# Gated attention and feed-forward decode: a piece of one wq block moves from the 128-partition stream to eight four-partition DMAs, and the stream's buffers get another start address

## The chip, the cores and the metric

The kernel runs on one core of a Trainium2 chip. A core has the engines PE (TensorE, matmul), DVE (VectorE), ACT (ScalarE), POOL (GpSimd) and SP (SyncE), and 16 DMA engines that bring data from device memory (HBM) to the core's memory (SBUF, 128 partitions). The metric is the time of one execution in device microseconds (us). The time before is 812.78 us, the median of 3 runs (812.65 to 812.88).

## The reference, cut to what matters

One token `x` of 1024 numbers goes through two branches, and a sigmoid gate mixes them. All numbers are float32.

```python
q = x @ wq                      # 1024 -> 32 heads of 128
scores = q @ k.T * 128 ** -0.5  # 4 kv heads, 65536 cached keys each; 8 query heads share a kv head
o = softmax(scores) @ v
a = o @ wo                      # 4096 -> 1024
y = (silu(x @ w_gate) * (x @ w_up)) @ w_down      # 1024 -> 3584 -> 1024
b = x + y * sigmoid(x @ w_r)
out = g * a + (1 - g) * b       # g = sigmoid(sum(x * gate_w))
```

Every weight and every cached key and value is used once, for one token: some 346 MB are read and 4 KB are written.

## The kernel before, in words

All large inputs are laid out on the host as one stream, in the order in which they are used: for each of the four kv heads g its part of wq (`q`), its keys, its values and its part of wo, then w_gate, w_up and w_down. In each of the 128 partitions the stream has `TOTAL` = 675,840 floats. It is cut into 48 loads: a first one of `FIRST` = 2048 columns, a tensor of its own (`flow0`), and 47 of `LOAD` = 14,336 columns (57,344 bytes in each partition, 7,340,032 bytes in all) from `flow`.

`at(part, first, n)` (L88) gives the SBUF columns that hold a stretch of the stream. When the load that holds it hasn't been asked for, it takes the next of the three buffers of the pool `stream` (L71) and issues the load on SP (L95 for the first, L99 for the others). A load into a buffer waits until PE has read all of the buffer's former content, so up to three loads are on the way or in use. SP issues nothing else but the store of the result (L293). The last two loads are cut into two and six pieces (`ENDS`, L51), so that PE can begin on the first columns.

A DMA of a load writes all 128 partitions. Between HBM and SBUF a partition's columns of one DMA are contiguous on both sides.

The work on a load is matmuls with the streamed data as the moving operand, 32 output rows at a time in four row groups j:

- `queries(g)` (L150): 8 blocks k of wq, 4 matmuls of 256 columns each (L154), with the columns of `xp` as weights. The result goes through `q_sb` (L159) and two small matmuls with `sel4` (L162) into `qp` (L164).
- `score_chunk` (L169): 16 matmuls of 512 columns for a chunk of 8192 keys (L173), ACT's copy (L178), DVE's maximum (L179). `neg_max` (L182) makes the softmax's offset from the 8 chunks, with a matmul of its own (L189).
- `value_chunk` (L197): ACT's exponential (L198), DVE's transpose (L200), 16 matmuls (L203). `project` (L208) scales and multiplies by wo (L226).
- `up_proj` (L242) for w_gate and w_up (L249), then w_down (L280, and L287 for the last block in two pieces), the last vector operation (L292) and the store.

The tile framework orders the instructions of each engine and sets the waits. The pool `const` holds the small tiles that live for the whole kernel; the three buffers of `stream` come behind it in each partition, so the size of `const` sets where they begin. The sizes in `const` are those of the tiles in the listing, each rounded up to 32 bytes: `xk` (L79) has 3 x 8 floats, 96 bytes. POOL does nothing but make `ident` (L106), from which DVE makes `sel`, `sel8`, `sel4` (L111 to L117). ACT issues the two small loads of `xk` and `x_row`; the latter writes four partitions, 0, 32, 64 and 96 (L84).

Of the kernel before, what the change touches and what calls it, by code (L numbers as in the profile page):

```python
# [1 line left out]

# [6 lines left out]
F32 = mybir.dt.float32  # L9
# [4 lines left out]
P = 128  # L14
D = 1024
G = 4
# [6 lines left out]
NM = CH // 512  # L23
NB = CH // P
KB = D // P
NQ = D // 4
FB = F // P
FQ = FB // 4
# [3 lines left out]
LOAD = 14336  # L32
PARTS = [("q", 0, KB * D)]
for _g in range(G):
    PARTS += [("k", _g, NCH * CH), ("v", _g, NCH * CH), ("o", _g, HG * D)]
    if _g < G - 1:
        PARTS.append(("q", _g + 1, KB * D))
PARTS += [("gate", 0, KB * F), ("up", 0, KB * F), ("down", 0, FB * D)]
BEGIN = {}
TOTAL = 0  # L40
# [1 line left out]
    BEGIN[_n, _g] = TOTAL  # L42
    TOTAL += _l

FIRST = TOTAL % LOAD
NLOAD = TOTAL // LOAD + 1
assert FIRST and (BEGIN["gate", 0] - FIRST) % LOAD == 0

PIECES = [(0, 192), (192, NQ)]

ENDS = {NLOAD - 2: [8 * D, LOAD], NLOAD - 1: [6 * D, 10 * D, 12 * D, 13 * D, 13 * D + 768, LOAD]}  # L51


@with_exitstack
def gated_mix_kernel(ctx: ExitStack, tc: tile.TileContext, x, vecs, flow0, flow, out):

# [10 lines left out]
    nc = tc.nc  # L69
    const = ctx.enter_context(tc.tile_pool(name="const", bufs=1))  # L70
# [5 lines left out]
    ps_1 = ctx.enter_context(tc.tile_pool(name="ps_1", bufs=1, space=bass.MemoryType.PSUM))  # L76


    xk = const.tile([P, 3, KB], F32, name="xk")  # L79
    nc.scalar.dma_start(xk, vecs)  # L80
    x_row = const.tile([P, NQ], F32, name="x_row")
    nc.vector.memset(x_row, 0.0)

    nc.scalar.dma_start(x_row.rearrange("(j r) n -> j r n", r=32)[:, 0, :], x.rearrange("(j n) -> j n", j=4))  # L84

    loads = []

    def at(part, first, n):  # L88

        i, a = divmod(BEGIN[part] + first - FIRST, LOAD)  # L90
        i, a = (i + 1, a) if i >= 0 else (0, BEGIN[part] + first)
        while len(loads) <= i:
            t = stream.tile([P, LOAD], F32, name="st", tag="st")
            if not loads:
                nc.sync.dma_start(t[:, :FIRST], flow0)  # L95
            else:
                ends = ENDS.get(len(loads), [LOAD])
                for c0, c1 in zip([0] + ends, ends):
                    nc.sync.dma_start(t[:, c0:c1], flow[len(loads) - 1, :, c0:c1])  # L99
            loads.append(t)  # L100
        return loads[i][:, a : a + n]

    at(("q", 0), 0, 1)

    ident = const.tile([P, P], F32, name="ident")
# [13 lines left out]

    xp = const.tile([P, KB, 32], F32, name="xp")  # L120
    nc.vector.memset(xp, 0.0)
    nc.vector.tensor_copy(xp[:, :, 0], xk[:, 0, :])

    qp = const.tile([P, 2, 4, 32], F32, name="qp")
    nc.vector.memset(qp, 0.0)
# [5 lines left out]

    dots = const.tile([P, 2, KB], F32, name="dots")
    for i in range(2):
# [3 lines left out]
    ps = ps_1.tile([P, P], F32, name="ps_m", tag="m")  # L137
# [5 lines left out]
    gate = sig[:, 0:1]  # L143
# [3 lines left out]
    nc.vector.tensor_mul(rest[:, 1:2], rest[:, 0:1], sig[:, 1:2])  # L147
    att = ps_1.tile([P, NQ], F32, name="att", tag="att")

    def queries(g):  # L150
        ps = ps_s.tile([P, 512], F32, name="ps_q", tag="s")
        for k in range(KB):
            for j in range(4):
                nc.tensor.matmul(  # L154
                    ps[32 * j : 32 * j + 32, :NQ], xp[:, k, :], at(("q", g), k * D + j * NQ, NQ),
                    start=(k == 0), stop=(k == KB - 1),
                )
        q_sb = work.tile([P, NQ], F32, name="q_sb")
        nc.vector.tensor_copy(q_sb, ps[:, :NQ])  # L159
        pt = ps_1.tile([P, P], F32, name="ps_m", tag="m")  # L160
        for e in range(2):
            nc.tensor.matmul(pt[:, 4 * e : 4 * e + 4], q_sb[:, e * DH : (e + 1) * DH], sel4, start=True, stop=True)  # L162
        for s in range(4):
            nc.vector.tensor_copy(  # L164
                qp[:, g % 2, s, 8 * s : 8 * s + 8].rearrange("p (j e) -> p e j", e=2),
                pt[:, :HG].rearrange("p (e j) -> p e j", e=2),
            )

    def score_chunk(g, c, mx):  # L169
        ps = ps_s.tile([P, 512], F32, name="ps_s", tag="s")  # L170
        for s in range(4):
            for j in range(4):
                nc.tensor.matmul(  # L173
                    ps[32 * j : 32 * j + 32, :], qp[:, g % 2, s, :], at(("k", g), c * CH + (4 * s + j) * 512, 512),
                    start=(s == 0), stop=(s == 3),
                )
        t = scores.tile([P, 512], F32, name="s", tag="s")
        nc.scalar.activation(t, ps, AF.Copy)  # L178
        nc.vector.tensor_reduce(mx[:, c : c + 1], t, AX.X, ALU.max)  # L179
        return t  # L180
# [50 lines left out]
    for g in range(G):  # L231
        queries(g)
        mx = work.tile([P, NCH], F32, name="mx")
        s_t = [score_chunk(g, c, mx) for c in range(NCH)]
        nb = neg_max(mx)
        sums = work.tile([P, NCH], F32, name="sums")
        acc = ps_o.tile([P, 512], F32, name="acc", tag="o")
        for c in range(NCH):
            value_chunk(g, c, s_t[c], nb, sums, acc)
        project(g, acc, sums)  # L240
# [37 lines left out]
    for b in range(FB - 1):  # L278
        for j in range(4):
            nc.tensor.matmul(  # L280
                y[32 * j : 32 * j + 32, :], hp[:, b, :], at(("down", 0), b * D + j * NQ, NQ),
                start=(b == 0), stop=False,
            )
    for c0, c1 in PIECES:
        n = c1 - c0
        for j in range(4):
            nc.tensor.matmul(  # L287
                y[32 * j : 32 * j + 32, c0:c1], hp[:, FB - 1, :], at(("down", 0), (FB - 1) * D + 4 * c0 + j * n, n),
                start=False, stop=(c1 == NQ),
# [39 lines left out]
```

## Time and profile before

| | |
|---|---|
| median of 3 runs | 812.78 us (812.65 to 812.88) |
| the profiled execution, its own time | 812.77 us |
| its span, first to last instruction | 811.0 us |
| instructions | 6755 |
| PE busy | 420.3 us (52%) |
| DVE busy | 64.3 us (8%) |
| ACT busy | 45.6 us (6%) |
| read from HBM | 346.05 MB |

The profile is a page on one execution, and views of its trace. The span leaves out 1.8 us of the execution's time at its ends. "DMA" with digits is the busy share of the 16 DMA engines in 40 slices, in tenths. A DMA queue is named by a number: q1 is SP's, q10 is ACT's, and two queues of kind "instruction" bring the engines' own instructions. The "chain that ended last" goes back from the last instruction, at each step to what released it. A table of windows gives, for each stretch of the span, the busy time of each engine, then the clock granted to PE, the mean busy share of the 16 DMA engines and the rate in GB/s.

### The profile page before, as it was taken

To read this page: it belongs to the slowest core of one execution; us is meant where nothing else is said; L and a number is where in the kernel's file an instruction comes from. 1 tells how busy PE (TensorE), PEld (TensorE's weight loads), DVE (VectorE), ACT (ScalarE), POOL (GpSimd) and SP (SyncE) were. 2 spreads that over 40 slices of the span, in tenths; PEclk is the share of its full clock that TensorE was granted. 3 is DMA by queue.
4 is the path that set the end of the run, shared out by engine and by line. 5 is a ranking of instruction groups with operands and counts; after the bars stand their busy time and mean duration, and the time that the engine had idled before them with its cause. 6 is when DMAs were issued, how large, how long until landed. Compare 5 with 4: busy or idle time off the path is not lost.

```text
span 811.0 us, 6755 instructions
## 1 busy us (share of the span) xinstructions
PE 420.3 (52%) x3142; PEld 127.3 (16%) x3142; DVE 64.3 (8%) x149; ACT 45.6 (6%) x101; POOL 0.7 (0%) x6
## 2 busy tenths in 40 slices
PE   1455454555445564345544545555555544575485
PEld 0111110113101011012110111121111111121132
DVE  2000110000000120000010101000000200000000
ACT  0000020000000020000000300000000200000000
POOL 0000000000000000000000000000000000000000
PEclk9967767678866686666776677767667766677677
DMA  9999999999999999999999999999999999999996
GB/s 415 405 453 419 438 434 424 448 410 448 428 430 439 425 442 422 436 436 422 441 431 436 428 430 436 425 438 442 424 434 428 430 436 427 445 422 436 426 423 276
DMA packets 7963, 346.47 MB, mean 427 GB/s; under 512 B 1016, under 2 KB 1152, under 8 KB 1408
## 3 DMA queue, kind: packets, MB, share of 16 engines
q1 hardware_dynamic: 7784, 346.04, 99.0%
q8 instruction: 24, 0.39, 0.2%
q10 hardware_dynamic: 152, 0.02, 0.0%
q14 instruction: 3, 0.02, 0.0%
HBM read 346.05 MB, written 0.00 MB: 427 GB/s over the span
## 4 chain that ended last, share of the span: by engine, by line
DMA 81%; PE 17%; DVE 1%; issue 0%; SPq 0%; ACT 0%; ACTq 0%
DMA st<-in_flow 81%; PE ps_s L173 7%; PE acc L203 6%; PE ps_f L249 1%; PE ps_q L154 1%; PE att L226 1%; PE ps_m L218 0%; SPq L99 0%; PE ps_m L162 0%; DVE o_sb L214 0%; DVE q_sb L159 0%; ACT s L198 0%; PE ps_m L189 0%; DVE pt L200 0%; DVE mx L179 0%
## 5 line engine op out<-in xcount | busy, mean ns | idle before, releaser
L173 PE MATMUL ps_s<-st,qp 128*32 128x512 f32 x1024 | 154.0, 765 | 150.4 <-DMA st<-in_flow 149.4
L203 PE MATMUL acc<-st,pt 128*32 128x512 f32 x1024 | 155.2, 768 | 140.6 <-DMA st<-in_flow 133.3
L173 PEld LDWEIGHTS ps_s<-st,qp 128*32 128x32 f32 x1024 | 38.2, 136 | 262.1 <-issue 149.1
L203 PEld LDWEIGHTS acc<-st,pt 128*32 128x32 f32 x1024 | 37.3, 136 | 250.7 <-issue 135.4
L178 ACT ACTIVATE s<-ps_s 128x512 f32<-128x512 f32 x32 | 19.1, 597 | 576.7 <-PE ps_s L173 576.7
L249 PE MATMUL ps_f<-st,xp 128*32 128x448 f32 x256 | 34.9, 715 | 26.0 <-DMA st<-in_flow 26.0
L179 DVE TENSOR_REDUCE mx<-s 128x1 f32<-128x512 f32 x32 | 22.0, 686 | 286.4 <-ACT s L178 286.4
L200 DVE STREAM_TRANSPOSE pt<-s 128x512 f32<-128x512 f32 x32 | 22.8, 712 | 191.9 <-PE acc L203 188.2
L154 PE MATMUL ps_q<-st,xp 128*32 128x256 f32 x256 | 23.3, 514 | 18.8 <-DMA st<-in_flow 18.8
L226 PE MATMUL att<-st,op 128*32 128x256 f32 x256 | 20.8, 487 | 13.7 <-DMA st<-in_flow 12.1
L198 ACT ACTIVATE s<-s,nb 128x512 f32<-128x512 f32 x32 | 22.6, 708 | 11.0 <-DVE nb L194 11.0
L280 PE MATMUL y<-st,hp 128*32 128x256 f32 x216 | 16.5, 472 | 5.4 <-DMA st<-in_flow 5.2
L249 PEld LDWEIGHTS ps_f<-st,xp 128*32 128x32 f32 x256 | 9.8, 140 | 50.2 <-issue 27.6
L154 PEld LDWEIGHTS ps_q<-st,xp 128*32 128x32 f32 x256 | 10.0, 144 | 30.7 <-DMA st<-in_flow 20.2
L226 PEld LDWEIGHTS att<-st,op 128*32 128x32 f32 x256 | 9.7, 139 | 23.3 <-DMA st<-in_flow 13.1
L280 PEld LDWEIGHTS y<-st,hp 128*32 128x32 f32 x216 | 7.9, 133 | 13.7 <-DMA st<-in_flow 7.2
L254 ACT ACTIVATE row<-ps_f 128x896 f32<-128x896 f32 x2 | 1.8, 917 | 142.1 <-PE ps_f L249 142.1
L214 DVE COPY o_sb<-acc 128x512 f32<-128x512 f32 x4 | 2.8, 692 | 78.5 <-PE acc L203 78.5
L216 PE MATMUL ps_m<-sel,lb 128*128 128x8 f32 x8 | 1.9, 304 | 10.8 <-DVE lb L212 10.6
L159 DVE COPY q_sb<-ps_q 128x256 f32<-128x256 f32 x4 | 1.7, 425 | 63.6 <-PE ps_q L154 63.6
L189 PE MATMUL ps_m<-md,ones 128*128 128x128 f32 x8 | 2.5, 406 | 8.0 <-DVE md L187 8.0
L218 PE MATMUL ps_m<-sel,o_sb 128*128 128x8 f32 x32 | 5.0, 285 | 2.5 <-DVE o_sb L214 2.5
(55 smaller groups left out, 46.1 us busy)
## 6 DMA issues: line engine op xcount, KB each, us to landing
st<-in_flow SPq DMA_DIRECT2D x45, 7168.0 KB, 42.2
st<-in_flow SPq DMA_DIRECT2D x2, 3072.0 KB, 41.7
st<-in_flow SPq DMA_DIRECT2D x1, 4096.0 KB
st<-in_flow SPq DMA_DIRECT2D x2, 1024.0 KB, 21.9
st<-in_flow SPq DMA_DIRECT2D x1, 2048.0 KB, 36.9
st<-in_flow SPq DMA_DIRECT2D x1, 512.0 KB, 39.7
st<-in_flow SPq DMA_DIRECT2D x1, 384.0 KB, 40.3
st<-in_flow SPq DMA_DIRECT2D x1, 128.0 KB, 34.3
```

The lines of the kernel that those rows point to most:

```text
L154: nc.tensor.matmul(ps[32 * j : 32 * j + 32, :NQ], xp[:, k, :], at(("q", g), k * D + j * NQ, NQ), start=(k == 0), stop=(k == KB - 1),)
L173: nc.tensor.matmul(ps[32 * j : 32 * j + 32, :], qp[:, g % 2, s, :], at(("k", g), c * CH + (4 * s + j) * 512, 512), start=(s == 0), stop=(s ...
L178: nc.scalar.activation(t, ps, AF.Copy)
L179: nc.vector.tensor_reduce(mx[:, c : c + 1], t, AX.X, ALU.max)
L198: nc.scalar.activation(t, t, AF.Exp, bias=nb, scale=SCALE, accum_out=sums[:, c : c + 1])
L200: nc.vector.transpose(pt, t)
L203: nc.tensor.matmul(acc[32 * j : 32 * j + 32, :], pt[:, 32 * m : 32 * m + 32], at(("v", g), c * CH + m * 512, 512), start=(c == 0 and m < 4 ...
L214: nc.vector.tensor_copy(o_sb, acc.rearrange("p (s d) -> p s d", s=4))
L218: nc.tensor.matmul(ps[:, HG : 2 * HG], o_sb[:, s, :], sel[:, HG * s : HG * s + HG], start=(s == 0), stop=(s == 3))
L226: nc.tensor.matmul(att[32 * j : 32 * j + 32, :], op[:, h, :], at(("o", g), h * D + j * NQ, NQ), start=(g == 0 and h == 0), stop=(g == G - ...
L249: nc.tensor.matmul(ps[32 * j : 32 * j + 32, e, :n], xp[:, k, :], at((part, 0), k * F + (2 * j + e) * n, n), start=(k == 0), stop=(k == KB ...
L280: nc.tensor.matmul(y[32 * j : 32 * j + 32, :], hp[:, b, :], at(("down", 0), b * D + j * NQ, NQ), start=(b == 0), stop=False,)
```

## The change: a piece of wq on its own DMAs, and the loads that follow from it

- Of the last kv head's `q`, the first 768 columns of the last block (k = 7) leave the stream: 768 floats in each of 128 partitions, 393,216 bytes. The stream's `TOTAL` is 675,072 then.
- They are folded on the host into the tensor `quarters`, with 4 x 768 floats for each of 32 rows: row p of wq's 128 stands in row 32 * q + r, slot h, with p = 32 h + 16 q + r. In SBUF it is the tile `quart`, 48 partitions of 12,288 bytes, of which rows 0 to 15 and 32 to 47 hold data. POOL sets it to zero first.
- Eight DMAs bring it, each four partitions, four apart (r, r + 4, r + 8, r + 12, and the same 32 further on), 49,152 bytes. SP issues one behind every third load: behind loads 3, 6 and so on up to 24.
- `queries(3)` has 12 matmuls on `quart` in 4 slots, with `xh` as weights, in place of 3 on the stream: 41 matmuls for 32.
- The loads are cut anew (`CUTS`): 2048 columns, then 14,336 each, and 13,568 in the one load that holds the last head's `q`, so that from w_gate on the cuts are where they were. There is one tensor `flow` for all loads, the first included, whose rows are now 57,344 bytes apart.
- `xk` has a fourth vector (128 bytes), and `quart` and `xh` (512 bytes) come to `const`: together 12,832 bytes. The buffers of `stream` begin 12,832 bytes further on, at multiples of 256 bytes.

```diff
+NH = 4
+NC = 768
-        PARTS.append(("q", _g + 1, KB * D))
+        PARTS.append(("q", _g + 1, KB * D - (NC if _g == G - 2 else 0)))
...
-FIRST = TOTAL % LOAD
-NLOAD = TOTAL // LOAD + 1
+CUTS = [0]
+while CUTS[-1] < BEGIN["q", G - 1]:
+    CUTS.append(CUTS[-1] + LOAD if len(CUTS) > 1 else 2 * D)
+CUTS.pop()
+CUTS.append(BEGIN["gate", 0] - (BEGIN["gate", 0] - CUTS[-1]) // LOAD * LOAD)
+while CUTS[-1] < TOTAL:
+    CUTS.append(CUTS[-1] + LOAD)
+NLOAD = len(CUTS) - 1
...
-    xk = const.tile([P, 3, KB], F32, name="xk")
+    xk = const.tile([P, 4, KB], F32, name="xk")
...
+    quart = const.tile([48, NH, NC], F32, name="quart")
+    nc.gpsimd.memset(quart, 0.0)
+    fours = [slice(32 * q + r, 32 * q + r + 13, 4) for q in range(2) for r in range(4)]
...
             t = stream.tile([P, LOAD], F32, name="st", tag="st")
-            if not loads:
-                nc.sync.dma_start(t[:, :FIRST], flow0)
-            else:
-                ends = ENDS.get(len(loads), [LOAD])
-                for c0, c1 in zip([0] + ends, ends):
-                    nc.sync.dma_start(t[:, c0:c1], flow[len(loads) - 1, :, c0:c1])
+            ends = ENDS.get(len(loads), [CUTS[len(loads) + 1] - CUTS[len(loads)]])
+            for c0, c1 in zip([0] + ends, ends):
+                nc.sync.dma_start(t[:, c0:c1], flow[len(loads), :, c0:c1])
             loads.append(t)
+            if len(loads) % 3 == 0 and fours:
+                rows = fours.pop(0)
+                nc.sync.dma_start(quart[rows], quarters[rows])
...
+    xh = const.tile([48, NH, 32], F32, name="xh")
+    nc.vector.memset(xh, 0.0)
+    nc.vector.tensor_copy(xh[:, :, 0], xk[:48, 3, :NH])
...
+        mms = []
+        if g == G - 1:
+            mms = [(j, xh[:, i, :], quart[:, i, j * NQ : (j + 1) * NQ]) for i in range(NH) for j in range(NC // NQ)]
         for k in range(KB):
-            for j in range(4):
-                nc.tensor.matmul(
-                    ps[32 * j : 32 * j + 32, :NQ], xp[:, k, :], at(("q", g), k * D + j * NQ, NQ),
-                    start=(k == 0), stop=(k == KB - 1),
-                )
+            held = NC if g == G - 1 and k == KB - 1 else 0
+            mms += [(j, xp[:, k, :], at(("q", g), k * D + j * NQ - held, NQ)) for j in range(held // NQ, 4)]
```

In the order of PE's instructions, ten of the twelve new matmuls stand behind the last scores of head 2, ahead of that head's `neg_max` matmul (L189 before), and two behind it.

More of the change, by code (lines that the diff above doesn't have):

```diff
@@ L1 @@
+from bisect import bisect
 from contextlib import ExitStack
@@ L43 @@
     TOTAL += _l
-FIRST = TOTAL % LOAD
-NLOAD = TOTAL // LOAD + 1
-assert FIRST and (BEGIN["gate", 0] - FIRST) % LOAD == 0
+CUTS = [0]
[5 more added lines that the diff above has]
+    CUTS.append(CUTS[-1] + LOAD)
+assert CUTS[-1] == TOTAL
+NLOAD = len(CUTS) - 1
 PIECES = [(0, 192), (192, NQ)]
@@ L54, in gated_mix_kernel @@
 @with_exitstack
-def gated_mix_kernel(ctx: ExitStack, tc: tile.TileContext, x, vecs, flow0, flow, out):
+def gated_mix_kernel(ctx: ExitStack, tc: tile.TileContext, x, vecs, quarters, flow, out):
     nc = tc.nc
@@ L84, in gated_mix_kernel @@
     nc.scalar.dma_start(x_row.rearrange("(j r) n -> j r n", r=32)[:, 0, :], x.rearrange("(j n) -> j n", j=4))
+    quart = const.tile([48, NH, NC], F32, name="quart")
+    nc.gpsimd.memset(quart, 0.0)
+    fours = [slice(32 * q + r, 32 * q + r + 13, 4) for q in range(2) for r in range(4)]
     loads = []
     def at(part, first, n):
-        i, a = divmod(BEGIN[part] + first - FIRST, LOAD)
-        i, a = (i + 1, a) if i >= 0 else (0, BEGIN[part] + first)
+        first += BEGIN[part]
+        i = bisect(CUTS, first) - 1
+        assert first + n <= CUTS[i + 1]
         while len(loads) <= i:
             t = stream.tile([P, LOAD], F32, name="st", tag="st")
-            if not loads:
-                nc.sync.dma_start(t[:, :FIRST], flow0)
-            else:
-                ends = ENDS.get(len(loads), [LOAD])
-                for c0, c1 in zip([0] + ends, ends):
-                    nc.sync.dma_start(t[:, c0:c1], flow[len(loads) - 1, :, c0:c1])
+            ends = ENDS.get(len(loads), [CUTS[len(loads) + 1] - CUTS[len(loads)]])
+            for c0, c1 in zip([0] + ends, ends):
+                nc.sync.dma_start(t[:, c0:c1], flow[len(loads), :, c0:c1])
             loads.append(t)
-        return loads[i][:, a : a + n]
+            if len(loads) % 3 == 0 and fours:
+                rows = fours.pop(0)
+                nc.sync.dma_start(quart[rows], quarters[rows])
+        return loads[i][:, first - CUTS[i] : first - CUTS[i] + n]
     at(("q", 0), 0, 1)
@@ L151, in queries @@
         ps = ps_s.tile([P, 512], F32, name="ps_q", tag="s")
+        mms = []
+        if g == G - 1:
+            mms = [(j, xh[:, i, :], quart[:, i, j * NQ : (j + 1) * NQ]) for i in range(NH) for j in range(NC // NQ)]
         for k in range(KB):
-            for j in range(4):
-                nc.tensor.matmul(
-                    ps[32 * j : 32 * j + 32, :NQ], xp[:, k, :], at(("q", g), k * D + j * NQ, NQ),
-                    start=(k == 0), stop=(k == KB - 1),
-                )
+            held = NC if g == G - 1 and k == KB - 1 else 0
+            mms += [(j, xp[:, k, :], at(("q", g), k * D + j * NQ - held, NQ)) for j in range(held // NQ, 4)]
+        js = [j for j, _, _ in mms]
+        for i, (j, xs, ws) in enumerate(mms):
+            nc.tensor.matmul(
+                ps[32 * j : 32 * j + 32, :NQ], xs, ws, start=(j not in js[:i]), stop=(j not in js[i + 1 :])
+            )
         q_sb = work.tile([P, NQ], F32, name="q_sb")
@@ L309, with quarter @@
     down[:, -1] = np.concatenate([last[:, :, c0:c1].reshape(P, -1) for c0, c1 in PIECES], axis=1)
-    vecs = np.stack([a[n].reshape(P, KB) for n in ("A_x", "gate_w", "B_w_r")], axis=1)
-    whole = {"q": wq, "k": k, "v": v, "o": wo, "gate": [a["B_w_gate"]], "up": [a["B_w_up"]], "down": [down]}
-    flow = np.empty((P, TOTAL), np.float32)
-    for n, g, l in PARTS:
-        flow[:, BEGIN[n, g] : BEGIN[n, g] + l] = whole[n][g].reshape(P, -1)[:, :l]
+    def quarter(t):
+        t = t.reshape(NH, 2, 16, KB, -1)[:, :, :, KB - 1, :NC].transpose(1, 2, 0, 3)
+        return np.concatenate([t[0], np.zeros_like(t[0]), t[1]])
+    vecs = np.stack([a[n].reshape(P, KB) for n in ("A_x", "gate_w", "B_w_r", "A_x")], axis=1)
+    vecs[:48, 3, :NH] = quarter(a["A_x"])[:, :, 0]
+    whole = {"q": wq, "k": k, "v": v, "o": wo, "gate": [a["B_w_gate"]], "up": [a["B_w_up"]], "down": [down]}
+    whole = {m: [t.reshape(P, -1) for t in ts] for m, ts in whole.items()}
+    whole["q"][-1] = np.delete(whole["q"][-1], np.s_[(KB - 1) * D : (KB - 1) * D + NC], axis=1)
+    whole = np.concatenate([whole[n][g] for n, g, _ in PARTS], axis=1)
+    flow = np.zeros((NLOAD, P, LOAD), np.float32)
+    for i, (c0, c1) in enumerate(zip(CUTS, CUTS[1:])):
+        flow[i, :, : c1 - c0] = whole[:, c0:c1]
     arrays = {
@@ L317 @@
         "vecs": vecs,
-        "flow0": flow[:, :FIRST],
-        "flow": flow[:, FIRST:].reshape(P, NLOAD - 1, LOAD).transpose(1, 0, 2),
+        "quarters": quarter(wq[G - 1]),
+        "flow": flow,
     }
```

## The prediction

> **What bounds the kernel now.** I read the page first, then the chain of waits in order of time, then windows over the stream and its end, and last the waits of SP.
>
> ```profile
> span 811.0 us, 6755 instructions
> PE 420.3 (52%) x3142; PEld 127.3 (16%) x3142; DVE 64.3 (8%) x149; ACT 45.6 (6%) x101; POOL 0.7 (0%) x6
> DMA  9999999999999999999999999999999999999996
> q1 hardware_dynamic: 7784, 346.04, 99.0%
> q8 instruction: 24, 0.39, 0.2%
> DMA 81%; PE 17%; DVE 1%; issue 0%; SPq 0%; ACT 0%; ACTq 0%
> ```
>
> The stream (q1) keeps the 16 DMA engines busy in every slice but the last; no compute engine is near its span. So what counts is when the last DMA engine has brought its share, and what follows that. The reader should also note q8: 24 packets of instructions, 0.39 MB, run on the same engines. 0.2% of 16 x 811.0 us is some 26 us, about 1.1 us for each packet.
>
> Chain of waits in order of time: start, duration, what.
>
> ```profile
> 49.08 42.81 DMA st<-in_flow
> ...
> 100.08 42.68 DMA st<-in_flow
> ...
> 253.19 42.13 DMA st<-in_flow
> ...
> 301.65 46.05 DMA st<-in_flow
> ...
> 358.56 40.00 DMA st<-in_flow
> ...
> 562.85 40.65 DMA st<-in_flow
> ...
> 611.88 42.48 DMA st<-in_flow
> ...
> 766.79 40.29 DMA st<-in_flow
> ```
>
> Each row ends where a load has landed from all 16 engines: 91.89, 142.76, 295.32, 347.70, 398.56, 603.50, 654.36 and, at the end of the stream, 807.08 us. From 91.89 to 142.76, from 347.70 to 398.56 and from 603.50 to 654.36 there are 50.86 us for three loads: 16.95 us for one. From 295.32 to 347.70 there are 52.38, or 1.52 us more. The slowest engine lost 1.5 us there in one piece and never made it up. That is near what one packet of q8 takes, and I read it as one.
>
> Windows of the end: PE, PEld, DVE, ACT, POOL busy, PE's clock, mean share of the DMA engines, GB/s.
>
> ```profile
> 1.65:802.00 800.35, 415.61 (x3066) 125.45 (x3070) 63.07 (x145) 45.58 (x101) 0.00 (x0) 0.72 1.00 432
> 801.00:802.00 1.00, 1.00 (x16) 0.43 (x12) 0.00 (x0) 0.00 (x0) 0.00 (x0) 0.50 0.94 367
> 802.00:803.00 1.00, 1.00 (x20) 0.43 (x16) 0.00 (x0) 0.00 (x0) 0.00 (x0) 0.86 0.76 292
> 803.00:806.00 3.00, 2.39 (x44) 0.90 (x32) 0.00 (x0) 0.00 (x0) 0.00 (x0) 1.00 0.50 202
> 806.00:807.00 1.00, 0.64 (x8) 0.16 (x8) 0.00 (x0) 0.00 (x0) 0.00 (x0) 1.00 0.38 136
> 807.00:808.00 1.00, 0.64 (x16) 0.33 (x16) 0.16 (x1) 0.00 (x0) 0.00 (x0) 1.00 0.00 0
> ```
>
> This is the row that the change lives on: from 803 to 806 the share stands at 0.50. Eight engines have finished, eight go on. Of the early half, 0.44 + 0.26 of a possible 0.50 + 0.50 is busy from 801 to 803, so it ends at 802.4 us on average and by 803 for its last; the late half ends at 806.8 on average and 807.08 for its last. The gap of the averages is 4.4 us. If the 24 packets of q8 fall on eight engines, three each at 1.52 us, they make 4.6 us. So I take the late half to be the engines that fetch instructions.
>
> **The change, part by part.**
>
> *Bytes off the stream.* 393,216 bytes leave it, 24,576 for each of 16 engines. One load gives an engine 7,340,032 / 16 = 458,752 bytes in 16.95 us, 27.06 bytes a ns. That is **-0.91 us on every engine**, and on the path as far as the late half sets the end.
>
> *The same bytes back, in four partitions at a time.* Eight DMAs of 49,152 bytes come back on the queue. If each of the four partitions goes to an engine of its own, and always to the same four, each of these gets 8 x 12,288 = 98,304 bytes. At 27.06 bytes a ns that is 3.63 us. For the other bound I take the small packets of the end:
>
> ```profile
> DMA packets 266, 0.78 MB, mean 195 GB/s; under 512 B 33, under 2 KB 108, under 8 KB 236
> ...
> q1 hardware_dynamic: 266, 0.78, 49.2%
> ```
>
> (window 802.9 to 806.9: 49.2% of 16 x 4.0 us is 31.5 us of engines for 0.78 MB, 24.8 bytes a ns.) 12 KB lies between, so 3.63 to 3.96 us. I take 3.7, nearer to the long rows. Four engines of the early half would then end at 802.4 - 0.91 + 3.7 = 805.2 on average, and at most at 803.0 - 0.91 + 3.96 = 806.05. The late half ends at 807.08 - 0.91 = 806.17. So the late half still ends last, with little to spare, and the end moves by the full 0.91 us. What this term rests on is that the four belong to the early half. No row names the engine of a packet. Following single packets in order of start, I did not find the four engines of `x_row`'s four-partition DMA among those with gaps for a fetch, as far as chains a few ns apart can be told from one another. That is why I take the early half, and why the other case keeps a chance.
>
> [...]
>
> *SP.* Eight more issues and what they wait for:
>
> ```profile
> L99 SPq DMA_DIRECT2D st<-in_flow x53: 327/328/432, 1.2 to 773.1; - x53
> ...
> SPq L99 <- DMA st<-in_flow: 337.1, 46, 13.3
> SPq L99 <- PE acc L203: 170.8, 18, 15.8
> ```
>
> 8 x 0.33 = 2.6 us on an engine that waits for hundreds; each stands right behind a load's issue, and the next load can't be issued for another 17 us. The first of them waits for POOL's zeroing of `quart`. What is queued behind it on SP is load 4, which isn't issued before 49.08 (the chain). POOL's zeroing has a small row to go by:
>
> ```profile
> masks.py:197 POOL MEMSET ident<- 128x128 f32 x1 | 0.2, 205 | 0.3 <-POOLq L322 0.3
> ...
> 10.28 0.36 DVE L111 TENSOR_REDUCE sel<-ident 128x32 f32<-128x128 f32 x1
> ...
> 28.48 0.58 PE L162 MATMUL ps_m<-sel,q_sb 128*128 128x4 f32 x4 [0.65 <-DVE q_sb L159]
> ```
>
> 3072 columns for 128: at most 24 x 0.205 = 4.9 us. `ident` comes that much later, about when DVE wants it at 10.28; its first user on PE is at 28.48. Nothing on the path.
>
> *PE.* 9 more matmuls.
>
> ```profile
> L154 PE MATMUL ps_q<-st,xp 128*32 128x256 f32 x256 | 23.3, 514 | 18.8 <-DMA st<-in_flow 18.8
> ...
> 441.03 24.59 SPq L99 DMA_DIRECT2D st<-in_flow  x2
> 449.56 5.88 PE L173 MATMUL ps_s<-st,qp 128*32 128x512 f32 x32 [8.60 <-DMA st<-in_flow]
> ```
>
> The row has two records for each of 128 matmuls, so 0.18 us each; 12 on `quart` are 2.2 us, behind the scores that begin at 449.56. They push the release of that buffer, and so a load's issue at some 465.3, by 2.2 us. Two more loads, 33.9 us of transfer, are queued then, less the lead of the early half; the buffer is back some 16 us after the landing, 18 then. Hidden; the cover would be gone at about 29 us.
>
> *The first load*, now 8 KB rows 57,344 bytes apart and not contiguous: 2048 of 675,072 columns, which take 2.4 us at the stream's rate. I bound it by a tenth of that on either side, 0.2 us, and take nothing. The *tail* behind the last landing (PE, one DVE operation, the store) is unchanged. From 803 to 807 PE is idle for 0.61 + 0.36 = 0.97 us, so it can follow landings 0.91 us earlier.
>
> *Where the buffers begin.* `xk`'s 32 bytes more and 12,800 others shift the start by 32 modulo 256, to a multiple of 256; so before it lay 224 bytes past one. All rows of the trace have the one start, so the price is bounded only. Below, nothing. Above, all of the fixed cost of a packet: the 233 packets at the end that aren't tiny have 3348 bytes on average; at 24.8 bytes a ns that is 135 ns and at 27.06 it is 124, so 11 ns a packet. An engine has 7784 / 16 = 486 packets less 54 tiny ones (one for each DMA), 432: 4.8 us at most. Between these ends I take nothing: the stream's bytes are nearly all in long rows, whose 27.06 bytes a ns are the row this is nearest to, and a fixed cost that every packet has needn't come from its start.
>
> **Sum.** The profiled execution took 812.77 us, its span 811.0, which is the median of 812.78 but for 0.01. 812.77 - 0.91 = **811.9 us**, -0.11%.
>
> **The rivals.**
>
> *A: the start address counts.* For it: it concerns every packet, and only this kernel's own start has been seen. Against: the long rows are so long that even 11 ns are half a per cent of them. From a gain of 0.8 us it shows: 811.9 - 0.8 = 811.1 down to 811.9 - 4.8 = 807.1; two thirds of the bound, 3.2 us, gives 808.7, and half, 2.4, gives 809.5.
>
> [...]
>
> *B, on the other side: one of the four engines is of the late half.* Then this engine gets 98,304 bytes where it already ends last: + 3.63 to 3.96 - 0.91, so 815.5 to 815.8 us. It decides as soon as one of the four ended later than 807.08 + 0.91 - 3.7 = 804.3 before. For it: no row names engines, and half of them are late. Against: the reading of single packets above.
>
> *C: the DMAs don't go to four fixed engines.* Spread evenly over 16 they give back the 0.91 us: 812.8. All on one engine, 393,216 bytes are 14.5 us, less the lead of 4.7 and the 0.91: + 8.9, 821.7.
>
> **How the numbers follow.** Forecast 0.58 (its own range 811.4 to 812.6: the first load, a margin of only 0.1 us for the four engines, and one instruction packet more or less on them). A 0.30, B 0.08, C 0.04, of which 0.03 is the even spread. 0.2% is 1.6 us, about what a measurement of this kernel can tell from no change. Faster by more than that is A's 0.30 and 0.01 of the forecast; slower is B and the rest of C, 0.09; within it 0.60. The range goes from 808.6 (two thirds of A's bound) to 812.7. It leaves out B, C, and A's far end, under 2 in 10.
>
> **What the changed profile should show.** In the windows of the last 6 us the share steps not from 1.00 to 0.50 but to about 0.75 first (four early engines done), and all end within 1.2 us of each other. Three loads still land 50.86 us apart; if A is right, that is 50.6 to 50.8 (24 rows by up to 11 ns), in the middle of the stream where `quart` has no part. If B is right the share falls to below 0.25 for some 3 us at the end. The prediction is wrong at its root if the gap of 4.4 us doesn't come from the instruction packets, so that other engines are late in the next run.

## The result, and the profile after

The changed kernel takes 809.4 us (median of 6 runs, 809.27 to 810.36) for 812.78 before: ratio 0.9961, 95% interval 0.9949 to 0.9973, 3.4 us or 0.42% faster. The profiled execution shown here is the slowest of the six, 810.36 us with a span of 807.8; what lies outside the span is 2.6 us in it and 1.8 in the others, so I compare inside the span. Times, ranges and ratios are of executions in the fast state; only other_parts had slow ones, two of twelve (826.10 and 845.32 us).

The page of the changed kernel answers to that of before almost line by line; DMA is as busy as it was, and q8 has as many packets:

```profile
span 807.8 us, 6804 instructions
q1 hardware_dynamic: 7848, 346.04, 99.1%
q8 instruction: 24, 0.39, 0.2%
DMA 82%; PE 16%; DVE 1%; issue 0%; SPq 0%; ACT 0%; ACTq 0%
```

The same bytes at the same busy share in less time: each engine moved its bytes faster. Where, the chain of waits shows (changed kernel; start, duration, what):

```profile
203.49 41.61 DMA st<-in_flow
...
252.96 43.31 DMA st<-in_flow
...
302.59 44.88 DMA st<-in_flow
...
560.96 40.14 DMA st<-in_flow
...
610.12 41.73 DMA st<-in_flow
...
661.13 41.45 DMA st<-in_flow
...
763.15 40.81 DMA st<-in_flow
```

The rows end at 245.10, 296.27 and 347.47, and at 601.10, 651.85, 702.58 and 803.96. From 601.10 on three loads take 50.75 and 50.73 us, where they took 50.86 before: 0.12 us for the 24 rows of each engine, 5 ns a row. Over the stream's 47 long loads that is 47 / 3 x 0.12 = 1.9 us. From 245.10 to 347.47, where one of the eight DMAs comes with every third load, three loads take 51.17 and 51.20: 0.45 us more, which is the price of 12,288 bytes (0.45 us at 27.06 bytes a ns). So I take it that by then the last to land are the four engines that carry those DMAs.

Windows over the end (changed kernel, columns as before):

```profile
797.00:799.00 2.00, 1.88 (x28) 0.75 (x20) 0.00 (x0) 0.00 (x0) 0.00 (x0) 0.81 0.95 398
799.00:802.00 3.00, 2.15 (x36) 1.10 (x40) 0.00 (x0) 0.00 (x0) 0.00 (x0) 1.00 0.78 323
802.00:803.00 1.00, 0.86 (x16) 0.26 (x8) 0.00 (x0) 0.00 (x0) 0.00 (x0) 1.00 0.73 290
803.00:804.00 1.00, 0.64 (x8) 0.16 (x8) 0.00 (x0) 0.00 (x0) 0.00 (x0) 1.00 0.35 128
804.00:805.00 1.00, 0.65 (x16) 0.32 (x16) 0.28 (x1) 0.00 (x0) 0.00 (x0) 1.00 0.00 0
```

The step from 1.00 to 0.50 has gone. Four engines end near 799, twelve go on together (0.78, 0.73) and end within the last 1.2 us. The last landing is at 803.96 for 807.08.

The single packets in the traces, one level below these views, tell who the late ones are. A row's packet begins some 3 ns before the one ahead of it on its engine ends, and every engine has the same sequence of sizes, so most engines can be followed from packet to packet. In the trace before, seven of the fourteen that I could follow have three packets of q8 each and end at 817.6 to 818.1 us on the trace's own clock; the seven without any end at 813.1 to 814.4. In the changed kernel the four with the eight DMAs have no packet of q8. They end at 814.3 to 815.3, the seven that I could follow with three such packets at 814.7 to 815.0, and the four with neither at 810.6 to 811.1.

### The profile page after: what moved, and what is told of

It is laid out like the page before. It is cut to its first block, busy times and chain, and to the rows that moved or that the text cites. A ratio compares the mean times of both kernels' runs of the same rounds, so it can differ in the third digit from the quotient of the medians.

```text
span 807.8 us, 6804 instructions
## 1 busy us (share of the span) xinstructions
PE 404.4 (50%) x3160; PEld 124.2 (15%) x3160; DVE 64.5 (8%) x151; ACT 45.6 (6%) x101; POOL 3.3 (0%) x7
## 4 chain that ended last, share of the span: by engine, by line
DMA 82%; PE 16%; DVE 1%; issue 0%; SPq 0%; ACT 0%; ACTq 0%
DMA st<-in_flow 82%; PE ps_s L201 6%; PE acc L231 6%; PE ps_q L183 1%; PE att L254 1%; PE ps_f L277 1%; SPq L115 0%; PE ps_m L246 0%; DVE o_sb L242 0%; PE ps_m L190 0%; DVE q_sb L187 0%; ACT s L226 0%; DVE pt L228 0%; PE y L315 0%; DVE mx L207 0%
## 5 line engine op out<-in xcount | busy, mean ns | idle before, releaser
L201 PE MATMUL ps_s<-st,qp 128*32 128x512 f32 x1024 | 144.9, 725 | 159.1 <-DMA st<-in_flow 158.2
L231 PE MATMUL acc<-st,pt 128*32 128x512 f32 x1024 | 150.6, 749 | 141.4 <-DMA st<-in_flow 134.7
L277 PE MATMUL ps_f<-st,xp 128*32 128x448 f32 x256 | 31.4, 654 | 29.3 <-DMA st<-in_flow 29.3
L226 ACT ACTIVATION_READ_ACCUMULATOR s<-s,nb 128x1 f32 x32 | 5.9, 186 | 0.0
## 6 DMA issues: line engine op xcount, KB each, us to landing
st<-in_flow SPq DMA_DIRECT2D x44, 7168.0 KB, 42.5
```

Source lines behind the costliest of these rows:

```text
L201: nc.tensor.matmul(ps[32 * j : 32 * j + 32, :], qp[:, g % 2, s, :], at(("k", g), c * CH + (4 * s + j) * 512, 512), start=(s == 0), stop=(s ...
L226: nc.scalar.activation(t, t, AF.Exp, bias=nb, scale=SCALE, accum_out=sums[:, c : c + 1])
L231: nc.tensor.matmul(acc[32 * j : 32 * j + 32, :], pt[:, 32 * m : 32 * m + 32], at(("v", g), c * CH + m * 512, 512), start=(c == 0 and m < 4 ...
L277: nc.tensor.matmul(ps[32 * j : 32 * j + 32, e, :n], xp[:, k, :], at((part, 0), k * F + (2 * j + e) * n, n), start=(k == 0), stop=(k == KB ...
```

## The experiments

Theory 1: two independent gains, the bytes moved to early engines (0.91 us) and the buffers' start (the rest). Theory 2: the start does nothing and the eight DMAs bring it all.

**The start alone** (align_only), the kernel before with 32 idle bytes in `const`:

```diff
+    pad = const.tile([P, 8], F32, name="pad")
+    nc.vector.memset(pad, 0.0)
     x_row = const.tile([P, NQ], F32, name="x_row")
```

> The kernel before with one idle tile of 32 bytes in const, so that the stream's buffers begin at multiples of 256 bytes and nothing else moves. Theory 1 (the start address slows every long row, and its part of the gain is the larger one): 810.3 us, 810.0 to 810.7; three loads land 50.73 us apart for 50.86, and the share of the DMA engines still stands at 0.50 for some 4 us at the end. Theory 2 (the address does nothing, the eight DMAs bring the whole gain): 812.8 us and 50.86.

810.51 us (810.34 to 810.66; ratio to before 0.9972, 0.9960 to 0.9983): 2.27 us faster with no byte moved. Four pieces of its chain of waits, and its end:

```profile
48.48 43.25 DMA st<-in_flow
...
609.52 43.05 DMA st<-in_flow
...
660.49 42.74 DMA st<-in_flow
...
715.68 38.42 DMA st<-in_flow
```

```profile
800.00:801.00 1.00, 0.63 (x16) 0.38 (x16) 0.00 (x0) 0.00 (x0) 0.00 (x0) 1.00 0.78 304
801.00:802.00 1.00, 1.00 (x27) 0.56 (x20) 0.00 (x0) 0.00 (x0) 0.00 (x0) 1.00 0.46 193
802.00:803.00 1.00, 0.52 (x12) 0.14 (x8) 0.00 (x0) 0.00 (x0) 0.00 (x0) 1.00 0.49 201
803.00:804.00 1.00, 0.94 (x16) 0.28 (x12) 0.00 (x0) 0.00 (x0) 0.00 (x0) 1.00 0.51 205
804.00:805.00 1.00, 0.64 (x9) 0.16 (x9) 0.00 (x0) 0.00 (x0) 0.00 (x0) 1.00 0.31 115
```

652.57 to 703.23 is 50.66 us, and the half-and-half end is still there: the rows got faster, the gap between the halves stayed. Theory 2 falls.

Not all steps are that short. From 91.73 to 754.10 the 39 loads take 662.37 us. The kernel before took 664.18 for them, from 91.89 to 756.07, where this row of its chain ends:

```profile
718.23 37.84 DMA st<-in_flow
```

That is 0.14 us for three loads and 2.2 for 47. The single packets add up to the same: a row of 57,344 bytes takes 2123.4 ns on average before and 2118.7 here, 1.7 us for the 360 rows of an engine; its other rows give 0.2 us; and a packet of q8 takes 1064 ns before and 930 here, 0.4 us for the three of a late engine. So some 2.3 us are accounted for, and with the aligned start the instruction packets are shorter too: in move_only, off64 and off128 below they take 1060 to 1076.

**The move alone** (move_only), the changed kernel with the start put back to 224 bytes past a multiple of 256:

```diff
+    pad = const.tile([P, 56], F32, name="pad")
+    nc.vector.memset(pad, 0.0)
     x_row = const.tile([P, NQ], F32, name="x_row")
```

> The changed kernel with an idle tile of 224 bytes in const, so that the buffers begin 224 bytes past a multiple of 256 as before. Theory 1: 811.9 us, 811.5 to 812.2, by the 0.91 us of bytes alone; three loads 50.86 us apart where quart has no part. Theory 2: 809.4 us, as the changed kernel.

811.87 us (811.79 to 813.09; ratio 0.9990, 0.9981 to 0.9999): 0.91 us faster than before. Two pieces of its chain from the part without `quart`'s DMAs, and its end:

```profile
611.45 42.26 DMA st<-in_flow
...
662.51 42.05 DMA st<-in_flow
```

```profile
803.00:805.00 2.00, 1.74 (x36) 0.66 (x24) 0.00 (x0) 0.00 (x0) 0.00 (x0) 1.00 0.74 295
805.00:806.00 1.00, 0.77 (x12) 0.16 (x8) 0.00 (x0) 0.00 (x0) 0.00 (x0) 1.00 0.49 178
```

The rows end at 653.71 and 704.56, 50.85 us apart as before. 0.74 up to the last us: twelve engines, as forecast. The two parts alone sum to 3.18 us; together they give 3.38. The 0.2 us between is not settled.

**Other starts** (off128, off64): the kernel before with idle tiles of 160 and 96 bytes, as in align_only.

> The kernel before with an idle tile of 160 bytes in const: buffers begin 128 bytes past a multiple of 256. Theory 1a (only multiples of 256 are free of the cost): 812.8 us or, if the cost goes by the bytes ahead of the start, between 810.5 and 812.8. Theory 1b (a smaller unit, 64 or 128, is enough): 810.5 us.

> The kernel before with an idle tile of 96 bytes in const: buffers begin 64 bytes past a multiple of 256. Theory 1a (multiples of 256 only): 812.8 us; if the cost goes by the bytes ahead of the start, nearer to 810.5 than the run at 128. Theory 1b (64 is enough): 810.5 us; if 128 is the unit, 812.8.

812.27 us (812.16 to 812.5) at 128, ratio 0.9994 (0.9985 to 1.0003); 812.38 us (812.28 to 812.5) at 64, ratio 0.9995 (0.9986 to 1.0004). Set against 810.51 at 0, a start at 64 costs 1.87, at 128 1.76 and at 224 2.27 us. It doesn't go by the bytes ahead of the start; of those tried, only the multiple of 256 is without the cost.

**The start in HBM** (source224): align_only, with `flow` read from 56 floats further on.

```diff
+    flow = flow[56:].rearrange("(i p c) -> i p c", p=P, c=LOAD)
...
```

> The kernel with aligned buffers alone (810.5 us), but in HBM the tensor flow begins with 56 floats more, so that every long row is read from 224 bytes past a multiple of 256 bytes of its tensor. If the cost is one of transfers whose start is off 256 on either side: 812.5 to 812.8 us. If it is one of writes into SBUF alone: 810.5 us.

810.40 us (810.27 to 810.68; ratio 0.9972, 0.9961 to 0.9983), the same as align_only (810.51). So the cost goes with the start of the writes into SBUF.

**More engines** (eight_parts): 1536 columns, twice the bytes, in eight DMAs of eight partitions.

```diff
-NH = 4
-NC = 768
+NH = 2
+NC = 1536
...
-    fours = [slice(32 * q + r, 32 * q + r + 13, 4) for q in range(2) for r in range(4)]
+    fours = [slice(32 * q + r, 32 * q + r + 29, 4) for q in range(2) for r in range(4)]
...
```

> The changed kernel with twice the bytes off the stream (1536 columns), in eight DMAs of eight partitions. If eight partitions go to eight engines and these are the early half, the late half loses another 24,576 bytes: 808.5 us, 808.2 to 808.8, and the share stays near 1 until the last 2 us. If one or more of the four engines that come in belong to the late half, they get 98,304 bytes and lose 24,576 more: 3.7 - 0.9 = 2.8 us later, 812.2 us.

812.0 us (811.9 to 813.14; ratio 0.9992, 0.9983 to 1.0000), the second case. Its end:

```profile
800.00:802.00 2.00, 1.22 (x24) 0.50 (x20) 0.00 (x0) 0.00 (x0) 0.00 (x0) 1.00 0.89 362
802.00:804.00 2.00, 1.73 (x32) 0.78 (x24) 0.00 (x0) 0.00 (x0) 0.00 (x0) 1.00 0.31 119
804.00:806.00 2.00, 1.65 (x24) 0.57 (x24) 0.00 (x0) 0.00 (x0) 0.00 (x0) 1.00 0.13 52
```

0.13 of 16 is two engines, alone for the last 2 us: so at least some of the four engines that come in are late ones, which got bytes on top. This is the prediction's rival B, made to happen.

**Twice the bytes on four engines** (four_double): the same columns in sixteen DMAs of four partitions, now also into partitions 16 to 31 and 48 to 63.

```diff
...
+    fours = [slice(16 * q + r, 16 * q + r + 13, 4) for q in range(4) for r in range(4)]
...
-            if len(loads) % 3 == 0 and fours:
+            if len(loads) % 3 != 1 and fours:
...
```

> The same 1536 columns in sixteen DMAs of four partitions. If four partitions always go to the same four engines, each of these gets 196,608 bytes, 98,304 more than in the changed kernel, less 24,576 of the stream: they end 2.8 us later and now set the end: 811.6 to 812.3 us, with the share at 0.25 for some 2 us. If the DMAs go to changing engines, 808.5 us.

822.87 us (816.9 to 825.35; ratio 1.0109, 1.0077 to 1.0141): neither. Windows of its stream:

```profile
40.00:130.00 90.00, 46.35 (x312) 12.02 (x312) 9.16 (x18) 9.92 (x23) 0.00 (x0) 0.70 1.00 427
130.00:207.00 77.00, 32.74 (x244) 9.56 (x236) 3.92 (x7) 0.00 (x0) 0.00 (x0) 0.67 1.00 379
207.00:340.00 133.00, 66.04 (x492) 18.75 (x484) 11.96 (x26) 10.53 (x24) 0.00 (x0) 0.73 1.00 434
340.00:430.00 90.00, 43.24 (x356) 14.00 (x356) 5.36 (x13) 1.79 (x3) 0.00 (x0) 0.69 1.00 425
```

The engines are busy throughout, and from 130 to 207 they move 379 GB/s. SP issues the DMAs 5 to 8 of the sixteen, those into partitions 16 to 31, between 82.71 and 156.82 us, and what is queued on it lands some 40 us later (the median of a long load is 42.5 in the changed kernel); 13 to 16, into 48 to 63, are issued from 308.42 to 374.17, which goes with the milder dip at 340 to 430. At a share of 1.00, 379 GB/s means that the rows themselves took longer, which more bytes on four engines wouldn't do. The edit had changed two things, bytes and partitions.

**The partitions alone** (other_parts): the changed kernel, its bytes moved to partitions 16 to 31 and 48 to 63.

```diff
...
-    fours = [slice(32 * q + r, 32 * q + r + 13, 4) for q in range(2) for r in range(4)]
+    fours = [slice(32 * q + 16 + r, 32 * q + r + 29, 4) for q in range(2) for r in range(4)]
...
```

> The changed kernel with the same eight DMAs writing partitions 16 to 31 and 48 to 63 in place of 0 to 15 and 32 to 47. Theory P (in the run with doubled bytes what hurt was not the bytes but that half of the DMAs wrote partitions 16 to 31 and 48 to 63: all long rows ran slower around just those): slower than 812, 812 to 822 us, with stretches at less than 400 GB/s around the eight DMAs. Theory Q (it was the bytes on four engines): 809.4 us, as the changed kernel.

813.57 to 824.79 us in ten executions (ratio 1.0057, 1.0030 to 1.0083). The partitions alone turn a gain of 3.4 us into a loss, and a steady time into a scattered one. Theory Q falls; of P's stretches under 400 GB/s the one kept trace, of 813.77 us, shows none: no fortieth of its span but the last is under 409.

**The grouping alone** (in_a_row): the changed kernel's own 32 partitions, four in a row to a DMA.

```diff
-    fours = [slice(32 * q + r, 32 * q + r + 13, 4) for q in range(2) for r in range(4)]
+    fours = [slice(32 * q + 4 * r, 32 * q + 4 * r + 4) for q in range(2) for r in range(4)]
```

> The changed kernel, the same bytes into the same 32 partitions, but each of the eight DMAs writes four partitions in a row (0 to 3, 4 to 7 and so on) and not four that lie four apart. [...] Theory P2 (partitions 16 to 31 and 48 to 63 are the trouble, whichever engine writes): 809.4 us.

816.23 us (816.07 to 816.52; ratio 1.0043, 1.0030 to 1.0056): slower, as with partitions 16 to 31, but not scattered; P2 falls. First two pieces of its chain, then one of the changed kernel's, then its end:

```profile
413.47 43.03 DMA st<-in_flow
...
770.26 40.28 DMA st<-in_flow
```

```profile
406.50 43.34 DMA st<-in_flow
```

```profile
802.00:804.00 2.00, 2.00 (x24) 1.02 (x20) 0.00 (x0) 0.00 (x0) 0.00 (x0) 0.50 0.74 310
804.00:806.00 2.00, 1.62 (x20) 0.50 (x16) 0.00 (x0) 0.00 (x0) 0.00 (x0) 0.65 0.74 300
806.00:808.00 2.00, 1.87 (x32) 0.87 (x32) 0.00 (x0) 0.00 (x0) 0.00 (x0) 1.00 0.26 109
808.00:810.00 2.00, 1.42 (x24) 0.57 (x24) 0.00 (x0) 0.00 (x0) 0.00 (x0) 1.00 0.22 90
```

A share of 0.26 is four engines alone, for some 4 us. The time is lost while the eight DMAs come: the load that lands at 449.84 us in the changed kernel lands at 456.50 here, and from there to the last landing the two take 354.12 and 354.04 us. 6.66 us over eight DMAs are 0.8 us for each.

The single packets show what is lost. In the changed kernel the 32 packets of 12,288 bytes take 460 ns each, and the long rows beside them 2116 ns on average. In this run the 32 take 588 on average and 1404 at most, and the rows beside a DMA 2209 to 2533 on average, from DMA to DMA. At each some 15 rows or more are lengthened, about one on every engine. In other_parts the 32 take 519 and the rows beside them 2295 to 2450. In four_double the rows beside the eight DMAs into partitions 0 to 15 and 32 to 47 take 2116, and those beside the other eight 2329 to 2966. So the placement slows the whole stream, not only the four engines.

in_a_row changes one thing more: its four rows lie next to each other in HBM, 12,288 bytes apart and not 49,152. other_parts kept that distance and was slow all the same, but for in_a_row this rival is not tested. What makes the grouping count was not shown.

**How much to move** (nc1024, nc512): 1024 or 512 columns for 768.

```diff
-NC = 768
+NC = 1024
```

> The changed kernel with 1024 columns for 768, in eight DMAs of four partitions to the same partitions: 131,072 bytes for each of the four engines. They lose 8,192 more of the stream and get 32,768 more, 1.21 - 0.30 = 0.91 us later; the late half ends 0.30 us sooner. Where the four engines now end with the late half, as the share of 0.72 to 0.78 up to the last us says, they set the end: 810.0 us, 809.7 to 810.3. If the DMAs' engines still had room, 809.1 us.

> The changed kernel with 512 columns for 768: 65,536 bytes for each of the four engines. If the late half sets the end at 768, it ends 0.30 us later here: 809.7 us. If the four engines set it at 768, they end 1.21 - 0.30 = 0.91 us sooner and the late half takes over: between 808.5 and 809.4.

810.45 us (810.29 to 810.83; ratio 0.9972, 0.9961 to 0.9983) and 809.69 us (809.46 to 810.2; ratio 0.9963, 0.9950 to 0.9977). Near the end, first 1024, then 512:

```profile
803.00:804.00 1.00, 0.83 (x16) 0.28 (x12) 0.00 (x0) 0.00 (x0) 0.00 (x0) 1.00 0.29 107
```

```profile
803.00:804.00 1.00, 1.00 (x20) 0.47 (x16) 0.00 (x0) 0.00 (x0) 0.00 (x0) 0.69 0.42 156
```

At 512 the late half sets the end (0.42 of 16 is more than four engines), 0.29 us later as worked out. At 1024 the four engines set it (0.29), 1.05 us later where 0.6 was the middle of what I expected. So 768 lies near where both ends meet; no version tried beats it.

## Why the prediction was right or wrong, point by point

The forecast was 811.9 us, with a range of its own of 811.4 to 812.6. 809.4 lies outside that, and inside the wide range of 808.6 to 812.7 only because this takes in two thirds of rival A's bound. What came is forecast and rival A together, and A had 0.30.

- **The bound** was right: the stream on the DMA engines, and of these the last eight. That these are the ones that bring the instructions, three packets each, was a guess from 4.4 and 4.6 us; the single packets show it for the seven of them that I could follow.
- **-0.91 us for the bytes off the stream** was right in move_only. That it agrees to the hundredth is luck, since the ratio's interval allows for 0.1 to 1.5 us. nc512's 0.29 us fits the same slope.
- **The same bytes on four engines of the early half, hidden by a small margin**: right but for the margin. That four partitions go to four engines, always the same, was an assumption; in the packets of the changed kernel the 32 of 12,288 bytes lie on four engines, eight on each. The price of a DMA shows in the chain, 0.45 us each or 3.6 in all for the 3.7 taken; the share of 0.74 in move_only and of 0.78 and 0.73 after and the packets show the four to be early ones. The forecast had them end 0.1 us ahead of the late half. In the profiled execution the last of them ends 0.4 us behind it, and nc1024, 1.05 us later, bears out that no room was left.
- **SP, PE, POOL at nothing**: right. An issue of `quart` took SP 0.60 us for the 0.33 forecast, hidden all the same. POOL's zeroing took 2.65 us, inside the bound of 4.9, and the twelve new matmuls fell into gaps of PE's (changed kernel, its issues and timeline):

```profile
L119 SPq DMA_DIRECT2D quart<-in_quarters x8: 599/602/758, 3.4 to 358.5; - x8
```

```profile
0.73 2.65 POOL L102 MEMSET quart<- 48x3072 f32 x1 [0.29 <-POOLq L358]
...
455.03 1.91 PE L183 MATMUL ps_q<-quart,xh 48*32 48x256 f32 x20
...
457.52 0.62 PE L183 MATMUL ps_q<-quart,xh 48*32 48x256 f32 x4
```

- **Where the buffers begin, taken at nothing**: this is the term that failed. It is worth 2.27 us by itself, the larger part of the gain, and lies inside the bound of 4.8; rival A with half of its bound gave 809.5, and 809.4 came, which is luck too: nothing spoke for the half. I set it to zero since the long rows run at 27.06 bytes a ns, the row it was nearest to. But those rows all had the one start: they couldn't speak for or against it, and their rate held the cost already. 0.14 us in 50.86 is too little to look like a cost without a second start to compare.
- **Not foreseen**: that it matters which four partitions a DMA writes; of the three placements tried only this one leaves the stream's rows alone (2116 ns beside the eight DMAs, for 2209 to 2533 in in_a_row and 2295 to 2450 in other_parts). I asked only which engines carry the bytes, and not where in SBUF they are written. That the changed kernel has the good placement made the forecast of this part come out, by luck.

## What to carry to other kernels

When a kernel is bound by one long stream, look at the last microseconds in narrow windows: a DMA share that stands at a half or a quarter names how many engines are late (here 0.50, eight of 16, from 803 to 806), and bytes can be moved to the others, up to the gap (here 4.4 us). Check the byte at which streamed buffers begin in SBUF; a small tile more ahead of them can shift it by 32 bytes; here that brought 2.27 of 812.78 us, 0.3%. When a small DMA runs beside the stream, choose its partitions as carefully as its size (here 809.4 or 816.23 us for the same bytes and partitions, grouped in two ways), and change one of the two at a time.

## What the runs showed of the hardware that I had not expected

- A start in SBUF 64, 128 or 224 bytes past a multiple of 256 costs 1.87, 1.76 and 2.27 us of 812, nearly alike; a start in HBM 224 bytes further on costs nothing (810.40 for 810.51).
- 393,216 bytes in eight small DMAs make the whole execution 6.8 us longer (816.23 for 809.4) with the same partitions in another grouping, and 4 to 15 us longer (813.57 to 824.79) with other partitions. The stream's own long rows beside such a DMA then take 2209 to 2533 ns for 2116. Why, and why the slow stretch in four_double (379 GB/s at a DMA share of 1.00) goes on between its DMAs, is open.
- In the kernel before, seven of the fourteen DMA engines that could be followed have three packets of instructions each, 1064 ns on average, and end some 4 us after the seven without any (817.6 to 818.1 us on the trace's own clock for 813.1 to 814.4). The share of 0.50 from 803 to 806 says that eight of the 16 are late.
